# Query-key products by pairs of feature groups, one evacuation of the modulation rows, and a new issue order in a fused attention and token-MLP kernel

## The chip, the cores and the metric

The kernel runs on one core of one Trainium2 chip. The time is the device time of one execution in microseconds (us); lower is better. Five engines take part: TensorE (matrix products; its weight loads are listed apart as PEld), VectorE (DVE), ScalarE (ACT), GpSimd (POOL) and SyncE (SP), which issues most of the DMA transfers.

## The reference

A block of two halves over 2048 tokens of 512 features, in bf16. A vector `c` gives six rows of 512 by `silu(c) @ w_mod`: shift, scale and gate of each half.

```python
h = layernorm(x) * (1 + ca) + sa
x = x + ga * A(h, wqkv, wo)
h = layernorm(x) * (1 + cb) + sb
x = x + gb * B(h, w1, b1, w2, b2)
```

A is attention with 32 heads of 16 features in a dilated window: each token looks at itself and at the tokens 2, 4, ... 14 positions before it, eight in all; positions before the start are masked. B is an MLP over the tokens: for each feature, the 2048 tokens go through `w1` (2048 to 1792), a GELU, and `w2` back to 2048.

## The kernel before

**Tiles.** The tokens are cut into five chunks of 2, 4, 4, 4 and 2 tiles of 128 (`SIZES`), 256 or 512 tokens each. For a chunk, `build_chunk` (line 634) makes:

- the layernorm and its transpose (`ln1s`, `rstd1`, `n1`, then `tr` and `hT` on TensorE, or `xt` by DMA for chunks 2 to 4);
- the projections `qkv{chunk}_{0 q, 1 k, 2 v}{group}` and their evacuations `ev` from PSUM. The 16 features of a head are split into four groups of four; a partition holds one head and one feature of a group, and one group's q, k or v is a row of all the chunk's tokens;
- the query-key products `qk{chunk}_{group}` (line 767): VectorE multiplies q with eight shifted views of k, 8 x 512 = 4096 elements (2048 in the small chunks), into one of four `big` buffers. TensorE sums four features at a time with the matrix `group4` (`red`, line 775) into `psL`. `red` frees the `big` buffer;
- the softmax: `max` on VectorE, `sub` on TensorE, `exp` on ScalarE, `esum` on TensorE, `rcp` on ScalarE, `smB` on VectorE. Then four small DMAs (`a2`) bring the weights to the layout of the values, of which `vd` DMAs make shifted copies (`vD`);
- the value products `pv` on VectorE, also into `big` buffers, their sums `pvacc` on TensorE, the evacuation `oev`, the output projection `wo` and the residual `x1`;
- the second layernorm: `ln2q`, `rstd2`, `n2`, then `aff` (line 903): two VectorE instructions that multiply by the row 1 + cb and add the row sb; then a third normalisation, `ln3s`, `rstd3`, `h3`, which is B's own.

The MLP's first matrix is cut into sweeps (`mlp1_{part}_{column tile}_{first token tile}`) that start as soon as the first tiles of `h3` are there; partial sums are parked in SBUF (`park`, `padd`). `gelu`, then `mlp2_{token tile}`, `fin` and the stores follow.

**Modulation rows.** `build_mod_rows` (line 588) multiplies `silu(c)` with the columns of `w_mod`, a single row first (`modrow0`, the gate ga) and then three (`modrow1`: sb, cb, gb). The evacuation `mrows1` is two VectorE instructions: a copy of the three rows, and cb once more with 1 added (line 610). The rows go to DRAM (`st_row`) and come back spread over the partitions (`ld_row`).

**The order.** All operations are recorded first and then issued in the order of the list `ORDER` (line 192). Each engine runs its own operations in this order, and SyncE its DMAs. A token may name the engine (`:a` ScalarE, `:d` VectorE, `:p` GpSimd, `:s` SyncE). `:q` on a matrix product makes `mm` (line 541) issue it as four products of 32 output rows that run side by side in column tiles of the array, where it would else be one product over the whole array. `red`, `pvacc` and `modrow` are always in such tiles, `mlp2`, `qvb` and the transposes never. `fill:n` are n products without use. PSUM buffers (`ps`, six) and `big` buffers are given out in `schedule` (line 86): a buffer is held from the operation that allocates it to the last that frees it, and the one that has been free longest is taken.

All instructions are issued by a helper, so the profile gives line 143 for nearly all of them; they are told apart by the names of their tiles.

Of the kernel before, what the change touches and what calls it, by code (L numbers as in the profile page):

```python
# [42 lines left out]
class _Graph:  # L43
# [42 lines left out]
    def schedule(self):  # L86
# [4 lines left out]
        for pos, token in enumerate(ORDER.split()):  # L91
# [22 lines left out]
            if o.alloc is not None:  # L114
                p = o.alloc.pool
                o.alloc.i = min((freed[p][k], k) for k in range(self.pools[p]) if held[p][k] is None)[1]
                held[p][o.alloc.i] = o.alloc
# [54 lines left out]
def _t_tt2(n):  # L172
    return 0.154 + 0.00052 * n
# [25 lines left out]
ln1s12:a ev0_02:d ln1v13 qk0_2 qk0_0 qk0_1 qk0_3 ld_wqkv2 ld_wrow3 ld_x_4_14 qkv1_13:q qvb1 qkv0_20 ev1_10:a wsc2_2:a  # L199
ev1_00:a ln1s14 ev1_13:a qkv1_03:q red0_0 qkv0_22:q ln1v12 rstd1_3 ev1_03:a qvb_cp1:a qkv1_11:q red0_1 red0_2 red0_3  # L200
mask ld_wrow0 ld_wmod2 ld_wrow2 modrow0 qkv1_01:q ld_wrow1 ld_b1 qk1_0 max0 sub0:q qk1_3 ev0_20:a ev0_22:a ev1_11:a
ev1_01:a exp0 wsc1_3:a halo_v1:a qkv1_12:q biascols:q qkv1_02 ev1_02:a esum0:q rcp0 mrows0:a ev1_12:a qk1_1 wsc0_1:p
wsc1_1:p wsc0_2:p n1_7:p n1_9:p wsc1_2:p n1_6:p smB0 qk1_2 wsc2_3:a qkv1_22:q red1_0 qkv1_21:q modrow1 wsc2_0:a
a2_0_1:a ev1_22:a ev1_21:a ln1s15 nb1_3 red1_1 qkv1_23:q red1_2 red1_3 mrows1 max1 xt6 xt8 qkv1_20:q ev1_23:a wsc2_1:a
ev1_20:a qkv2_00:q qkv2_10:q vd0_2 vd0_3 vd0_1 ld_wo2 vd0_0 st_row0 a2_0_2:s a2_0_3:s a2_0_0:s ld_wo3 ld_row0 ld_wo0
n1_11:p n1_10:p pv0_1 pv0_2 pv0_3 pv0_0 sub1:q ev2_00:a biascols_cp:a exp1 ev2_10:a qkv2_03:q pvacc0_2 qkv2_11:q
fill:6:q qkv2_13:q esum1:q pvacc0_3 n1_12:a n1_13:a ev2_13:a ev2_03:a oev0_2:a pvacc0_0 pvacc0_1 rcp1 rstd1_4 oev0_0:a
qk2_0 woq_s smB1 qk2_3 qkv2_01:q qkv2_12:q qkv2_02:q ev2_11:a ev2_01:a a2_1_1:a ev2_12:a ev2_02:a qk2_1 qk2_2 wo1:q
x1_1:a wo0:q x1_0:a ln2q1 xt10 xt12 red2_0 qkv2_23:q qkv3_22:q qkv3_12:q vd1_0 st_row1 vd1_2 ev2_23:a ln2q0 rstd2_0
nb1_4 nb2_0 qkv2_21:q ev2_21:a red2_1 a2_1_2:s a2_1_0:s a2_1_3:s vd1_1 ld_row1 vd1_3 n1_14:p pv1_2 qkv3_13:q red2_2  # L210
red2_3 max2 qkv2_22:q n1_15:a ev3_13:a n2_1:a ev3_12:a ev2_22:a n2_0:a halo_v2:p qkv2_20:q sub2:q ev2_20:a exp2
pvacc1_2 qkv3_10:q halo_v3:a oev1_2:a ev3_10:a qkv3_02:q qkv3_20:q pv1_1 qkv3_01:q pvacc1_1 esum2:q ev3_02:a ev3_20:a
ev3_22:a aff0 pv1_0 qkv3_03:q qkv3_00:q pvacc1_0 pv1_3 oev1_1:a ev3_01:a rcp2 halo_k3:a smB2 ln3s0 qkv3_11:q oev1_0:a
pvacc1_3 ev3_11:a oev1_3:a qkv3_23:q fill:1:q wo5:q wo3:q qk3_2 qk3_1 ld_w1_0_0 ld_w1_0_512 vd2_3 xt14 vd2_2 vd2_1
a2_2_1:s a2_2_0:s a2_2_2:s vd2_0 a2_2_3:s wo4:q ln3s1 ev3_03:a ev3_00:a qk3_0 x1_3:a x1_4:a qk3_3 ln2q3 ln2q4 x1_5:a
ev3_23:a qkv4_22:q qkv3_21:q ev3_21:a wo2:q red3_0 x1_2:a qkv4_20:q fill:2:q red3_1 qkv4_00:q red3_2 ev4_22:a ln2q5
ln2q2 ev4_20:a rstd2_2 pv2_0 rstd2_4 red3_3 pvacc2_0 oev2_0:a pv2_3 qkv4_12:q ev4_12:a qkv4_02:q nb2_2 ev4_02:a n2_2:a
max3 sub3:q pvacc2_3 exp3 esum3:q oev2_3:a rstd3_0 pv2_2 nb2_4 pvacc2_2 qkv4_10:q rcp3 n2_5:a oev2_2:a n2_4:a pv2_1
pvacc2_1 fill:4:q oev2_1:a wo6:q wo7:q wo8:q wo9:q ev4_00:a smB3 n2_3:p vd3_3 ld_w1_0_896 vd3_1 vd3_0 a2_3_2:s a2_3_3:s
a2_3_0:s a2_3_1:s vd3_2 ld_w2_1 aff2 nb3_0 aff4 h3_1:p h3_0:p halo_v4:p ln3s3:a ln3s2:d ln3s4:d ln3v3 ln3v2 ln3v4  # L220
ln3s5:a ln3v5 pv3_1 x1_8:a x1_7:a x1_6:a rstd3_2 ev4_10:a h3_3 h3_2 mlp1_0_1_0 mlp1_0_2_0 mlp1_0_5_0:q mlp1_0_3_0:q
pvacc3_1 rstd3_4 nb3_4 x1_9:a pv3_2 pv3_3 pv3_0 h3_4:a h3_5:a oev3_1:a mlp1_0_2_2:q mlp1_0_1_2:q mlp1_0_0_0:q
mlp1_0_0_2:q mlp1_0_3_2:q mlp1_0_0_4:q mlp1_0_5_2:q mlp1_0_5_4:q mlp1_0_3_4:q mlp1_0_1_4:q pvacc3_2 mlp1_0_2_4:q ln2q9
ln2q6 park0_0:a park0_1:a ln2q7 park0_2:a oev3_2:a qk4_0 qk4_2 mlp1_0_4_0:q mlp1_0_4_2:q pvacc3_3 mlp1_0_6_0:q ln2q8
oev3_3:a mlp1_0_6_2:q pvacc3_0 mlp1_0_6_4:q mlp1_0_4_4:q oev3_0:a mlp1_0_7_0:q wo13:qn red4_0 rstd2_6 nb2_6 park0_3:a
qk4_1 x1_13:d n2_9:a n2_6:a park0_4:a wo12:q n2_8:p ld_w1_0_1152 ld_w1_0_1408 vd4_1 ld_w2_3 vd4_2 vd4_0 vd4_3 n2_7:d
qk4_3 wo11:q red4_1 red4_2 red4_3 ln2q13 x1_12:a ln2q12 park0_5:a x1_11:a rstd2_12 aff6 ln3s7:a mlp1_0_9_0 mlp1_0_9_2
mlp1_0_8_0 mlp1_0_9_4 wo10:n max4 nb2_12 sub4 exp4 park0_6:a ln3s9:d ln3s8:d ln3v8 ln3v9 esum4 ln3s6:d ln3v7 rcp4 ln3v6
smB4 rstd3_6 mlp1_0_7_2 mlp1_0_8_2 mlp1_0_10_0 mlp1_0_10_2 mlp1_0_12_0 mlp1_0_12_2 mlp1_0_8_4 mlp1_0_10_4 mlp1_0_7_4
mlp1_0_12_4 a2_4_1:s a2_4_2:s a2_4_3:s n2_13:p x1_10:d nb3_6 h3_8:d h3_6:d h3_7:d a2_4_0:a h3_9:a ln2q10 ln2q11  # L230
rstd2_10 n2_12:d aff12 mlp1_0_11_0 mlp1_0_11_2 mlp1_0_11_4 mlp1_0_8_6 mlp1_0_7_6 pv4_1 nb2_10 pv4_2 pv4_0 ln3s13
mlp1_0_9_6 mlp1_0_10_6 park0_7:a park0_8:a n2_10:a park0_9:a park0_10:a mlp1_0_12_6 mlp1_0_11_6 pvacc4_0 pvacc4_1
# [21 lines left out]
def kernel(  # L254
# [29 lines left out]
    INJ=(1,),  # L284
    CENT=((0, 14), (2, 0), (2, 12)),
# [44 lines left out]
    big_r = ring(NBIG, [P, NW * CM], BF, "big")  # L330
# [16 lines left out]
    epscol = T([P, 1], F32, "epscol")  # L347
    a1col = T([P, KT], F32, "a1col")
# [149 lines left out]
    def mk_consts():  # L498
        nc.gpsimd.memset(group4[:], 1.0)
# [88 lines left out]
    def build_mod_rows():  # L588
        for b_, (r0, nr) in enumerate(((0, 1), (1, 3))):
# [488 lines left out]
```

## Time and profile before

| | |
|---|---|
| Time, median of 3 runs | 199.04 us (198.99 to 199.58) |
| Profiled execution | 198.75 us |
| Its span, first to last instruction | 197.0 us |
| Mean granted TensorE clock | 0.997 |
| Matrix products / VectorE / ScalarE / GpSimd instructions | 2331 / 222 / 304 / 46 |
| Moved by DMA | 36.02 MB |

The span is what the profile shows; the time of the execution is 1.75 us longer. A busy TensorE isn't TensorE at its peak, since products are pipelined and their ends modelled. In a timeline row stand the start, the duration from the first start to the last end, the engine, the operation with its tiles and the count of instructions merged; in brackets is the idle time ahead of it and what ended it.

### The profile page before, as it was taken

Reading aid. Unit: us, or ns where it says so; the run is one execution under the profiler, and the core shown is the slowest. Engines: PE = TensorE matmul, PEld = TensorE weight load, DVE = VectorE, ACT = ScalarE, POOL = GpSimd, SP = SyncE. Lnnn points to the kernel's source line nnn. Section 1 sums busy time; section 2 is a strip of 40 time slices with the busy share of each in tenths; the row PEclk is TensorE's granted clock in tenths of the full one; section 3 lists DMA queues with packets and bytes.
Section 4 is the critical chain, followed back from the end, with each engine's and each line's share of the span. In section 5 each row is a group of like instructions: output and inputs, shape, how many; then the busy total and the mean of one; then the engine's idle time right before and its main releaser. Section 6 shows DMA issues by size and latency. Waiting matters only on the chain.

```text
span 197.0 us, 5568 instructions
## 1 busy us (share of the span) xinstructions
PE 185.8 (94%) x2331; PEld 99.5 (50%) x2343; DVE 157.3 (80%) x222; ACT 127.1 (64%) x304; POOL 22.8 (12%) x46
## 2 busy tenths in 40 slices
PE   3999999999999996899999999999999999999993
PEld 1476656565465674435554454444444444444462
DVE  2789999999999999999999999977550207864693
ACT  4799999898999999999997899735660000000000
POOL 4184003000500001130031000500000000000000
PEclk9999999999999999999999999999999999999998
DMA  5999695888997449180497494588999200144113
GB/s 156 357 355 341 226 259 137 101 201 253 302 303 268 149 144 322 34 218 14 136 245 208 91 255 97 157 273 177 290 348 339 61 0 15 38 130 99 53 53 107
DMA packets 53893, 36.02 MB, mean 183 GB/s; under 512 B 24428, under 2 KB 50668, under 8 KB 53868
## 3 DMA queue, kind: packets, MB, share of 16 engines
q1 hardware_dynamic: 52772, 35.27, 64.2%
q10 hardware_dynamic: 1096, 0.39, 0.8%
q8 instruction: 18, 0.29, 0.6%
q14 instruction: 7, 0.06, 0.1%
HBM read 22.55 MB, written 2.10 MB: 125 GB/s over the span
## 4 chain that ended last, share of the span: by engine, by line
PE 63%; DVE 21%; issue 5%; DMA 4%; SPq 3%; ACT 2%; DVEq 0%; ACTq 0%
PE psS L143 61%; DVE big L143 14%; DMA xx<-in_A_x_dram 4%; DVE h L143 4%; SPq L143 3%; PE psL L143 2%; DVE lsb L143 1%; DVE st L143 1%; ACT xx L143 1%; ACT junk L143 1%; DVE m L143 1%; DVE nb L143 0%; ACT k_f L143 0%; DVE woq L143 0%; ACT rs L143 0%
## 5 line engine op out<-in xcount | busy, mean ns | idle before, releaser
L143 PEld LDWEIGHTS <-wst 128*128 128x128 bf16 (+1 forms) x578 | 35.6, 101 | 32.7 <-issue 2.8
L143 PE MATMUL psS<-h,wst 128*32 128x512 bf16 (+1 forms) x350 | 50.1, 379 | 0.4 <-issue 0.2
L143 DVE TENSOR_TENSOR big<-a2sb,vD 128x4096 bf16<-128x4096 bf16 (+1 forms) x20 | 36.4, 1857 | 0.1
L143 DVE TENSOR_TENSOR big<-q_sb,k_f 128x4096 bf16<-128x4096 bf16 (+1 forms) x20 | 36.3, 1857 | 0.0
L143 PE MATMUL psS<-hT,w_qkv 128*32 128x512 bf16 (+1 forms) x576 | 29.0, 344 | 0.0
L143 DVE SCALAR_TENSOR_TENSOR h<-psS,bcol,rows_bc 128x512 f32<-128x512 f32 (+2 forms) x17 | 12.1, 709 | 21.2 <-PE psS L143 21.0
L143 PEld LDWEIGHTS <-w_qkv 128*32 128x32 bf16 (+1 forms) x618 | 21.2, 107 | 13.9
L143 PE MATMUL psS<-gT,big 128*128 128x512 bf16 x111 | 24.8, 379 | 0.1
L143 POOL TENSOR_SCALAR h<-xx,rs,nb 128x512 bf16<-128x512 bf16 x11 | 11.5, 1047 | 94.3 <-DVE nb L143 40.6
L143 PEld LDWEIGHTS <-big 128*128 128x128 bf16 x144 | 12.1, 98 | 13.8 <-DMA big<-in_w_mod_dram 0.5
L143 PE MATMUL psS<-woq,o_sb 128*32 128x512 bf16 (+1 forms) x220 | 16.7, 379 | 0.3 <-ACT o_sb L143 0.3
L143 ACT ACTIVATE gT<-psS,bcol 128x512 bf16<-128x512 f32 x14 | 8.9, 685 | 8.6 <-DVE psS L143 8.6
L143 DVE TENSOR_TENSOR psS<-psS,gT 128x512 f32<-128x512 f32 x14 | 9.4, 697 | 5.5 <-PE psS L143 5.5
L143 DVE TENSOR_TENSOR h<-h,xx 128x512 bf16<-128x512 f32 (+2 forms) x17 | 11.1, 652 | 2.6 <-DMA out_dram<-h 2.1
L143 PE MATMUL psS<-hT,wst 128*32 128x512 bf16 (+2 forms) x134 | 11.8, 355 | 0.2
L143 DVE TENSOR_TENSOR h<-h,rows_bc 128x1024 bf16<-128x1024 bf16 (+2 forms) x16 | 11.5, 718 | 0.5
L143 ACT ACTIVATE v_sb<-psS,qvb 128x512 bf16<-128x512 f32 (+1 forms) x20 | 11.1, 599 | 0.7 <-PE psS L143 0.7
L143 DVE BATCH_NORM_STATS2 st<-xx 128x6 f32<-128x512 bf16 x12 | 7.9, 681 | 4.5 <-DMA xx<-in_A_x_dram 4.5
L143 PEld LDWEIGHTS <-group 128*32 128x32 bf16 x288 | 7.7, 96 | 7.3 <-DVE big L143 1.7
L143 PE MATMUL psS<-big,group 128*32 128x512 bf16 (+1 forms) x160 | 9.9, 338 | 1.1 <-DVE big L143 0.8
L143 ACT ACTIVATE q_sb<-psS,qvb 128x512 bf16<-128x512 f32 (+1 forms) x18 | 10.6, 614 | 0.4 <-PE psS L143 0.3
L143 PEld LDWEIGHTS <-o_sb 128*32 128x32 bf16 (+1 forms) x220 | 7.0, 97 | 7.1 <-ACT o_sb L143 0.8
(106 smaller groups left out, 249.3 us busy)
## 6 DMA issues: line engine op xcount, KB each, us to landing
vD<-v_sb SPq DMA_DIRECT2D x12, 524.5 KB, 5.1
big<-in_B_w_dram SPq DMA_DIRECT2D x4, 896.0 KB, 8.3
vD<-v_sb SPq DMA_DIRECT2D x8, 268.5 KB, 2.5
wst<-in_B_w_dram SPq DMA_DIRECT2D x3, 640.0 KB, 4.4
out_dram<-h SPq DMA_DIRECT2D x15, 128.0 KB, 1.8
wst<-in_B_w_dram SPq DMA_DIRECT2D x2, 800.0 KB, 5.4
xx<-in_A_x_dram SPq DMA_DIRECT2D x6, 256.0 KB, 7.2
gT<-in_w_mod_dram SPq DMA_DIRECT2D x4, 384.0 KB, 7.6
```

The source lines that it names most:

```text
L143: r = fn(*a, **k)
```

## The change

- `qk` now takes two feature groups in one VectorE instruction (`QKP`, all chunks): 8192 elements in the chunks of 512 tokens, 4096 in the small ones. `big` becomes two double buffers, and a pair of the large chunks holds both halves of one until both its `red` are done. `schedule` gives out aligned pairs. The products are stored window by window with all tokens of the chunk in a row, so that `red` reads four runs of a window apart.
- `modrow1` gets four more products, ones times the identity, which add 1 to cb in PSUM; `mrows1` is one copy, and the order puts it on ScalarE.
- `aff` becomes two operations, `afm` (multiply) and `afs` (add), which the order can set apart.
- `ORDER` is new from chunk 0's query-key products on; the part before is unchanged. Tokens of ten `qk` instead of twenty stand in it. Among those that change engine: `mrows1` from VectorE to ScalarE; `ev0_20` and `wsc2_2` from ScalarE to VectorE; `n1_6`, `n1_7`, `n1_11`, `n1_14` from GpSimd to ScalarE; `n2_7` and `n2_9` to GpSimd. Other products have the `q` flag than before. The fillers behind the unchanged part are 26 units, before 13.

```diff
-                    held[o.frees.pool][o.frees.i] = None
-                    freed[o.frees.pool][o.frees.i] = pos
+                    z, k = o.frees.size, o.frees.i
+                    held[o.frees.pool][k:k + z] = [None] * z
+                    freed[o.frees.pool][k:k + z] = [pos] * z
...
+    QKP=(0, 1, 2, 3, 4, ),
+    PVP=(),
...
-    big_r = ring(NBIG, [P, NW * CM], BF, "big")
+    big_t = ring(NBIG // 2, [P, 2, NW * CM], BF, "big")
+    big_r = [big_t[i // 2][:, i % 2, :] for i in range(NBIG)]
...
+                    if (r0, r) == (1, 1):
+                        for dt_ in range(KT):
+                            nc.tensor.matmul(ps(s_)[32 * dt_:32 * dt_ + 32, r * P:(r + 1) * P],
+                                             lhsT=ones[:, 0:1].to_broadcast([P, 32]), rhs=ident[:], start=False, stop=True,
+                                             tile_position=(0, 32 * dt_))
...
-            if nr == 1:
-                copy2(rows, src_, P, False, [], [("mrows", b_)], f"mrows{b_}", frees=s_)
-            else:
-                def f_cp(rows=rows, src_=src_):
-                    nc.vector.tensor_copy(rows, src_())
-                    nc.vector.tensor_scalar_add(rows[:, 1, :], src_()[:, 1, :], 1.0)
-                add("dve", 0.8, f_cp, writes=[("mrows", b_)], frees=s_, name=f"mrows{b_}")
+            copy2(rows, src_, nr * P, False, [], [("mrows", b_)], f"mrows{b_}", frees=s_)
...
-        for dlo in range(4):
-            s_ = _Slot("big")
+        NQ = 2 if ch in QKP else 1
+        for d0 in range(0, 4, NQ):
+            s_ = _Slot("big", NQ * C // CM or 1)
...
+                return _ap(big_t[s_.i // 2][:, s_.i % 2, 0:1], [[NW * C, NQ], [C, NW], [1, C]])
+
+            def f(d0=d0, prod=prod):
+                qv = _ap(q_sb[:, d0, 0:1], [[C, NQ], [0, NW], [1, C]])
+                k0, k1 = k_c[:, 0, PAD:PAD + 1], k_c[:, 1, PAD:PAD + 1]
+                kv = _ap(k_c[:, d0, PAD:PAD + 1], [[k1.offset - k0.offset, NQ], [-DIL, NW], [1, C]])
+                nc.vector.tensor_tensor(prod(), qv, kv, op=ALU.mult)
...
+                            nc.tensor.matmul(psL[32 * jj:32 * jj + 32, hf, 0:WPM * SB], lhsT=group4[:],
+                                             rhs=pr[:, hf * WPM:(hf + 1) * WPM, jj * SB:(jj + 1) * SB], start=(dlo == 0),
+                                             stop=(dlo == 3), tile_position=(0, 32 * jj))
...
-                nc.vector.tensor_tensor(hv, hv, ab_bc[:].unsqueeze(1).to_broadcast([P, gn, D]), op=ALU.mult)
-                nc.vector.tensor_tensor(hv, hv, sb_bc[:].unsqueeze(1).to_broadcast([P, gn, D]), op=ALU.add)
+            for nm, row, rk, op_ in (("afm", ab_bc, "ab_bc", ALU.mult), ("afs", sb_bc, "sb_bc", ALU.add)):
```

The parts of the new order that the prediction speaks of, from the start of what changed, around the first MLP products, and around chunk 4's softmax:

```diff
+ln1s12:a ev0_02:d ln1v13 qk0_0 qk0_2 ld_wqkv2 ld_wrow3 ld_x_4_14 qkv1_01:q ev1_00:a n1_7:a qvb1 ev1_01:a qvb_cp1:a
+n1_6:a qkv0_20:q qkv0_22:q ev0_22:a qkv1_11:q red0_0 red0_1 red0_2 red0_3 mask ln1v12 rstd1_3 ev1_10:a ev1_11:a
+ev0_20:d wsc1_2:p n1_9:p wsc0_1:p wsc0_2:p wsc1_1:p wsc1_3:p nb1_3 wsc2_2:d max0 ld_wrow2 ld_wo0 ld_wrow0 ld_wmod2
+ld_wrow1 ln1s14 xt6 vd0_3 xt8 ld_wo2 ld_b1 vd0_0 vd0_1 qkv1_13:q sub0:q qkv1_02:q qkv1_03:q exp0 esum0:q modrow0
+qkv1_12:q ev1_02:a rcp0 ev1_13:a ev1_03:a mrows0:a st_row0 ev1_12:a qk1_0 smB0 qk1_2 qkv1_22:q n1_11:a qkv1_20:q
+qkv1_23:q a2_0_2:a ln1s15 red1_0 qkv2_11:q qkv1_21:q ev1_23:a ev2_11:a ev1_21:a n1_12:a ev1_22:a ev1_20:a red1_1
+qkv2_10:q red1_2 modrow1 red1_3 qkv2_00:q qkv2_01:q halo_v1:p n1_13:a wsc2_3:a ev2_10:a ev2_01:a n1_10:p a2_0_0:s
+a2_0_1:s a2_0_3:s vd0_2 ld_row0 ld_wo3 xt10 xt12 pv0_3 pv0_1 max1 sub1:q qkv2_13:q pv0_0 exp1 pvacc0_0 pvacc0_1 esum1:q
...
+vd3_3 ln3s3:a nb3_0 h3_1:p h3_0:p afs4 ln3s2:d ln3s4:d ln3v3 ln3v4 ln3v2 x1_7:a rstd3_2 x1_6:a ln3s5:a pv3_1 h3_3 h3_2
+ln3v5 mlp1_0_1_0 mlp1_0_2_0 mlp1_0_5_0 pvacc3_1 pv3_2 x1_9:a x1_8:a oev3_1:a rstd3_4 nb3_4 h3_5:d h3_4:a ln2q9 pv3_3
...
+nb2_6 n2_8:a n2_6:a park0_4:a park0_5:a mlp1_0_6_4:q mlp1_0_8_0:q red4_0 qk4_2 park0_6:a red4_1 wo13:qn mlp1_0_7_0:q
+mlp1_0_8_2:q red4_2 red4_3 x1_13:d wo12:q max4 sub4:q ln2q13 exp4 wo11:qn n2_7:p n2_9:p afm6 esum4 x1_12:a ln2q12 wo10
```

More of the change, by code (lines that the diff above doesn't have):

```diff
@@ L115, in schedule @@
                 p = o.alloc.pool
[L116 to L117 removed]
+                z = o.alloc.size
+                o.alloc.i = min((max(freed[p][k:k + z]), k) for k in range(0, self.pools[p] - z + 1, z)
+                                if held[p][k:k + z] == [None] * z)[1]
+                held[p][o.alloc.i:o.alloc.i + z] = [o.alloc] * z
             if o.frees is not None:
@@ L203 @@
[L203 to L207, printed above, removed]
@@ L218 @@
[L218 to L222, printed above, removed]
@@ L223 @@
[L223 to L232, printed above, removed]
```

111 lines of the change are left out of this document (59 added, 52 removed).

## The prediction

> **What bounds the kernel now.** I read the page first, for the engines' shares and the slices, then the chain of work that ended last in order of time, and then the busy times of each stretch that the chain separates.
>
> ```profile
> PE 185.8 (94%) x2331; PEld 99.5 (50%) x2343; DVE 157.3 (80%) x222; ACT 127.1 (64%) x304; POOL 22.8 (12%) x46
> ...
> DVE  2789999999999999999999999977550207864693
> ```
> ```profile
> 68.39 6.36 DVE big L143 x3
> ...
> 88.13 0.49 ACT k_f L143
> ...
> 88.67 10.66 PE psS L143 x192
> ```
> ```profile
> 16.50:39.90 23.40, 23.34 (x527) 14.06 (x531) 22.90 (x24) 22.18 (x51) 2.02 (x3) 1.00 0.78 207
> 39.90:62.00 22.10, 21.89 (x444) 12.44 (x440) 22.07 (x17) 21.02 (x49) 2.94 (x2) 1.00 1.00 266
> 62.00:88.67 26.67, 23.38 (x529) 14.02 (x522) 26.47 (x25) 25.83 (x70) 3.21 (x4) 1.00 0.60 182
> 88.67:117.00 28.33, 28.23 (x341) 14.30 (x346) 27.82 (x43) 25.84 (x65) 2.46 (x2) 1.00 0.61 148
> 150.00:190.50 40.50, 40.29 (x186) 18.41 (x189) 21.02 (x30) 0.00 (x0) 0.00 (x0) 1.00 0.26 77
> ```
>
> The columns of the stretches are the length, then busy time of PE, PEld, DVE, ACT and POOL, the granted clock and the DMA share. TensorE looks like the bound at 94%, but that is an average over two halves. From 16.5 to 88.67 us, the attention, VectorE is busy for 22.90 + 22.07 + 26.47 = 71.44 of 72.17 us, and the last stretch leaves TensorE 3.3 us of holes. From 88.67 us on, the token MLP, the chain stays on TensorE until 190.5 us. So the time is: the moment at which VectorE lets TensorE into the MLP, plus the TensorE work behind that moment, plus a tail that the change doesn't touch. ScalarE, at 25.83 of 26.67 us, has no room either. I take as the gate the first product of chunk 3's values (pv3_1) and the matmuls that sum it (pvacc3_1), since both orders have them there.
>
> **VectorE up to the gate.** The prices are start to start, because consecutive instructions overlap by some 0.07 us.
>
> ```profile
> 17.46 4.63 DVE L143 TENSOR_TENSOR big<-q_sb,k_f 128x2048 bf16<-128x2048 bf16 x4
> ...
> 32.10 0.55 DVE L143 CAST mrows<-psS 128x384 bf16<-128x384 f32 x1
> 32.69 0.29 DVE L143 TENSOR_SCALAR mrows<-psS 128x128 bf16<-128x128 f32 x1
> 33.26 1.22 DVE L143 TENSOR_REDUCE m<-psL 128x128 bf16<-128x1024 f32 x1 [0.28 <-PE psL L143]
> ...
> 61.65 8.89 DVE L143 TENSOR_TENSOR big<-q_sb,k_f 128x4096 bf16<-128x4096 bf16 x4
> ```
> ```profile
> L143 DVE TENSOR_TENSOR big<-q_sb,k_f 128x4096 bf16<-128x4096 bf16 x12 | 26.9, 2282 | 0.0
> ...
> L143 DVE TENSOR_SCALAR h<-xx,rs,nb 128x512 bf16<-128x512 bf16 x5 | 2.1, 411 | 0.1
> ...
> L143 DVE TENSOR_TENSOR q_sb<-psS,qvb 128x512 bf16<-128x512 f32 x1 | 0.7, 691 | 0.0
> ```
>
> Four products of 4096 elements take 8.89 us, so one starts (8.89 - 2.28) / 3 = 2.20 us after the last; of 2048, taking 1.22 us for the last one, (4.63 - 1.22) / 3 = 1.14. The 2048 more elements cost 1.06, so the fixed part is 1.14 - 1.06, about 0.07 us. That is all that a pair saves: elements are not fewer, and a pair of 4096 should take 4.34 us against 4.41. No row shows 8192 elements; the bounds are 0 and 0.15 us per pair (0.15 by whole durations: 2 x 1.22 - 2.28, rounded down), and I take 0.07, the row of back-to-back instructions. Eight pairs stand before the gate: **-0.56**. The second evacuation (mrows1) leaves VectorE, from 32.10 to 32.69 + 0.29 = 32.98: **-0.85** with its gaps. In return the order gives VectorE ev0_20, by the evacuation of the same form 0.69 - 0.07 = **+0.62**, and wsc2_2, a 512-element scaling at 0.41 - 0.07 = **+0.34**. One small aggregate (ln3v5) goes behind the gate, some **-0.1**. The split of aff into afm and afs has the same two instructions. Sum: **-0.55 us**. The 0.28 us that the maximum of chunk 1 waits should go too, since two value products of chunk 0 now lie before it.
>
> mrows1 lands on ScalarE at about the 0.55 of its cast, and four normalisations move there from GpSimd, while ev0_20, two weight scalings, one normalisation and a halo copy leave. Summed by durations less overlap, the queue is within 1 us of its old length at each softmax, so I put it at nothing; without VectorE's cover it would cost up to that 1 us. The added identity products are four, of 128 columns, side by side: under 0.1 us.
>
> **What waits instead.** Two places of the new order look late.
>
> ```profile
> 22.61 1.03 PE L143 MATMUL psS<-hT,wst 128*32 128x512 bf16 x16
> 23.47 0.82 PE L143 MATMUL psL<-big,group 128*32 128x512 bf16 x12
> 24.22 0.23 PE L143 MATMUL psL<-mask,ident 32*32 32x128 bf16 x1
> ```
> ```profile
> 24.48 0.69 DVE L143 TENSOR_REDUCE m<-psL 128x64 bf16<-128x512 f32 x1
> ...
> 29.49 0.42 DVE L143 TENSOR_TENSOR lsb<-lsb,rb 128x512 bf16<-128x512 bf16 x1
> ...
> 34.55 4.63 DVE L143 TENSOR_TENSOR big<-a2sb,vD 128x2048 bf16<-128x2048 bf16 x4
> ```
> ```profile
> 29.25 0.56 SPq L143 DMA_DIRECT2D scratch<-mrows  x1
> 29.94 2.01 SPq L143 DMA_DIRECT2D a2sb<-lsb  x3
> ```
> ```profile
> a2sb<-lsb SPq DMA_DIRECT2D x6, 32.0 KB, 3.6
> ```
>
> First, max0 needs TensorE's mask product. TensorE has one projection group less ahead of it (23.47 - 22.61 = 0.86 us), so max0 can start at 24.48 - 0.86 = 23.6. VectorE, which used to put a product of chunk 1 in between, now arrives at 17.46 + 2 x 2.20 + 0.14 + 0.62 + 0.08 + 0.34 = 23.0. Wait: 0 to 0.6, I take **+0.5**. The whole of chunk 1's first pair is behind it. Second, pv0 needs the softmax of chunk 0 through a DMA. smB0 ends at 23.6 + 0.61 + 4.34 + 0.42 = 29.0. SyncE first issues st_row0 (0.56) and then three of the four pieces at 0.67 each, so the third issue starts at 30.9 at the latest, or at 30.3 if st_row0 is out before. Landing takes 3.6 us by the median, but before it took at most 34.55 - 31.28 = 3.3 us, as pv0 did not wait there: 33.6 to 34.2. VectorE is there after one pair, at 33.3, where the old order still had three more instructions. Wait: 0 to 1.0, I take **+0.4**; behind it wait max1 and everything of chunk 1. So up to the gate -0.55 - 0.28 + 0.5 + 0.4 = **+0.07**.
>
> **TensorE behind the gate.**
>
> ```profile
> 88.67 0.61 PE L143 MATMUL psS<-big,group 128*32 128x512 bf16 x8 [0.29 <-ACT k_f L143]
> 89.21 4.50 PE L143 MATMUL psS<-h,wst 128*32 128x512 bf16 x80
> 93.52 0.62 PE L143 MATMUL psS<-big,group 128*32 128x512 bf16 x8
> ...
> 101.51 0.83 PE L143 MATMUL psL<-big,group 128*32 128x512 bf16 x12
> 102.28 1.90 PE L143 MATMUL psS<-h,wst 128*128 128x512 bf16 x7
> ```
>
> A step of 512 columns in four column tiles takes (93.52 - 89.21) / 20 = 0.215 us. Before, four first MLP products stood ahead of pvacc3_1; now three do, and mlp1_0_3_0, two steps, goes behind: **+0.43**. The order also changes which products run in column tiles (the q flags). Three groups from 101.51 would end at 101.51 + 0.645 = 102.16, and the next, full-array product starts at 102.28: a change of form costs 0.12. Counted in the two orders, there are 3 changes behind the gate before and 7 after; one of these falls into the wait at the gate, so 3 x 0.12 = **+0.36** (0 to 0.5). The ten further changes ahead of the gate, 1.2 us, and 13 more filler units go into TensorE's 3.3 us of holes; without these they'd be paid.
>
> The Trainium skill, TensorEngine Tiling (Array Packing), section Key Properties, says that a change of tiling mode drains TensorE. By that rule the last product's whole 0.38 us would have to pass, 0.165 more than a step, an estimate of 0.5 in place of 0.36; the row shows the smaller price.
>
> ```profile
> wst<-in_B_w_dram SPq DMA_DIRECT2D x2, 800.0 KB, 5.4
> ```
>
> The tightest load of the MLP, ld_w1_2_0 of this size, has 5.4 us to landing; its buffer comes free with mlp1_1_5_10, and 29 steps of 0.215, 6.2 us, lie between that and its first use. It costs nothing, with 0.8 us of cover. The tail keeps its last two output tiles in the same order: nothing. Sum: +0.07 + 0.43 + 0.36 = **+0.86**. The profiled execution took 198.75 us (span 197.0 and 1.75 around it) and would come to 199.6; against the median of the runs, 199.04, I predict **199.9 us**.
>
> **The rivals.**
>
> ```profile
> 76.20 0.62 PE L143 MATMUL psL<-m,nident 128*32 128x512 bf16 x8 [1.04 <-DVE m L143]
> ...
> 78.05 0.63 PE L143 MATMUL psS<-lsb,ident 128*32 128x128 bf16 x32 [0.80 <-ACT lsb L143]
> ...
> 80.68 0.61 PE L143 MATMUL psS<-big,group 128*32 128x512 bf16 x8 [0.69 <-DVE big L143]
> ```
> ```profile
> 49.79 2.28 DVE L143 TENSOR_TENSOR big<-a2sb,vD 128x4096 bf16<-128x4096 bf16 x1
> ```
> ```profile
> 49.96 2.76 POOL L143 TENSOR_SCALAR h<-xx,rs,nb 128x512 bf16<-128x512 bf16 x1 [16.09 <-ACT v_sb L143]
> ...
> 104.87 0.77 POOL L143 TENSOR_SCALAR h<-xx,rs,nb 128x512 bf16<-128x512 bf16 x1 [4.66 <-DVE nb L143]
> ```
> ```profile
> L143 ACT ACTIVATE junk<-xx,sums 128x512 bf16<-128x512 bf16 x14 | 10.1, 723 | 0.2
> ```
>
> *Faster: the lead reaches the gate.* The two waits don't come, which is so if the softmax pieces land within a pair, 4.3 us, of smB0. Then VectorE gains 0.55 + 0.28 = 0.83, and TensorE, let in that much earlier, has done the moved steps and the changes in its holes of 1.04, 0.80 and 0.69 us: 199.04 - 0.83 = 198.2. If half of the two longest holes closes as well, 0.9 less, 197.3. For it speaks that these holes are there; against it that VectorE, not the order of TensorE, makes them.
>
> *No change.* The waits come, and TensorE's 0.79 us disappears in holes, or the other way about: 199.1 or 199.0. That the pairs don't do what they say belongs here too: at no saving per pair the forecast would move by 0.56, to 200.5. That they'd lose the fast rate I leave out: their innermost step stays one element of bf16, as in the products with vD, which cost the same 2.28.
>
> *Slower still: GpSimd behind a pair.* GpSimd's normalisation at 49.96 took 2.76 us while VectorE's product of 2.28 ran, against 0.77 at 104.87. In the new order n2_7 and n2_9 of chunk 2 both go to GpSimd just as VectorE starts the second pair of chunk 4 (2.20 us), and afm6 needs both: 2.20 + 2 x 0.77 = 3.7 us after the start, where VectorE arrives after 2.20 + 0.61 + 0.61 = 3.4. That 0.3, and the 0.72 us of a ScalarE square (ln2q11) that now stands ahead of h3_8, hit h3_6 to h3_9, which TensorE takes as soon as they are made: +1.0, so 200.9. It decides from the point where h3_8 comes later than mlp1_0_7_6 reaches it. The Trainium skill, SBUF — State Buffer, section SBUF: two separate sides, has the rule for this: the port pair that VectorE and GpSimd share is an exclusive lock for a whole instruction. The two rows above agree with it.
>
> **How the numbers follow.** Forecast 199.9: 0.34. Faster, 198.2: 0.33. No change, 199.1: 0.17. Slower still, 200.9: 0.16. The lower end takes in the faster case with most of the closed holes, 197.4; the upper end the slower case with half a microsecond more for the softmax pieces (1.0 in place of 0.4, rounded down), 201.4. Within 0.3% (0.6 us) is what a measurement of this kernel can't tell from no change; 0.05 of the forecast's chance falls in there. So faster 0.33, same 0.17 + 0.05 = 0.22, slower 0.29 + 0.16 = 0.45.
>
> **What would show it.** Each step has its place in the new profile: pairs at 4.34 us start to start; VectorE idle before the first maximum and before the first product with vD, by TensorE and by a DMA; the gate near 88.7 us; TensorE's work behind the gate longer by 0.8 us. I'm wrong if the gate opens before 88 us, or if TensorE's stretch behind it is as long as before; GpSimd's case shows as TensorE idle between 105 and 115 us.

## The result, and the profile after

The changed kernel takes **201.54 us** (median of 4 runs, 201.14 to 202.04) against 199.01 for the kernel before (198.44 to 199.58): ratio 1.0128, 95% interval 1.0091 to 1.0165. A second set of six runs gave 201.56 us and 1.0114 (1.0094 to 1.0134). Three executions of all that follow, at a lower granted clock, took over 1.5% longer than the fastest of the same kernel, and times and ratios leave them out. The forecast, 199.9, had the direction; the loss is three times as large, and 201.54 lies outside the range. The profiled execution of after took 201.54 us, 2.79 more than that of before.

The page of after, shares of the engines (VectorE has 11 instructions fewer, TensorE 35 more):

```profile
PE 188.0 (94%) x2366; PEld 97.4 (49%) x2366; DVE 156.4 (78%) x211; ACT 125.6 (63%) x298; POOL 24.7 (12%) x49
```

Busy times of after in the first stretch, columns as in the prediction:

```profile
16.50:39.90 23.40, 21.64 (x497) 13.37 (x499) 21.20 (x20) 20.41 (x46) 3.14 (x6) 1.00 0.91 203
```

In before VectorE was busy for 22.90 of these 23.40 us; now it has 2.2 us of holes. VectorE's own rows (start, duration, idle ahead of it) show the largest of these and the largest of a later stretch:

```profile
18.02 4.47 DVE L146 TENSOR_TENSOR big<-q_sb,k_f 128x4096 bf16<-128x4096 bf16 x2
...
23.93 0.69 DVE L146 TENSOR_REDUCE m<-psL 128x64 bf16<-128x512 f32 x1
24.53 4.42 DVE L146 TENSOR_TENSOR big<-q_sb,k_f 128x8192 bf16<-128x8192 bf16 x1
28.86 0.42 DVE L146 TENSOR_TENSOR lsb<-lsb,rb 128x512 bf16<-128x512 bf16 x1
...
35.69 2.40 DVE L146 TENSOR_TENSOR big<-a2sb,vD 128x2048 bf16<-128x2048 bf16 x2 [1.86 <-DMA a2sb<-lsb]
...
42.55 0.68 DVE L146 TENSOR_TENSOR lsb<-lsb,rb 128x1024 bf16<-128x1024 bf16 x1
...
63.71 8.75 DVE L146 TENSOR_TENSOR big<-q_sb,k_f 128x8192 bf16<-128x8192 bf16 x2
...
83.44 0.69 DVE L146 TENSOR_TENSOR lsb<-lsb,rb 128x1024 bf16<-128x1024 bf16 x1 [0.79 <-ACT rb L146]
```

The pairs do what was said: 8.75 - 4.42 = 4.33 us start to start. The first value product (pv0_3) waits 1.86 us for the softmax pieces, and smB3 0.79 us for ScalarE. SyncE's queue says why the pieces are late:

```profile
22.10 2.20 SPq L146 DMA_TRANSPOSE hT<-h  x1
24.49 0.63 SPq L146 DMA_DIRECT2D vD<-v_sb  x1
25.22 1.32 SPq L146 DMA_TRANSPOSE hT<-h  x1
26.59 0.69 SPq L146 DMA_DIRECT2D woq<-in_A_wo_dram  x1
27.33 0.56 SPq L146 DMA_DIRECT2D b_t<-in_B_b_dram  x1
27.94 2.10 SPq L146 DMA_DIRECT2D vD<-v_sb  x2
30.14 0.56 SPq L146 DMA_DIRECT2D scratch<-mrows  x1
30.81 2.86 SPq L146 DMA_DIRECT2D a2sb<-lsb  x3
```
```profile
L146 SPq DMA_DIRECT2D a2sb<-lsb x3: 617/685/1448, 30.8 to 32.2; - x3
```

From 22.10 us on it has no gap: seven entries, 7.50 us in all, ahead of the row's store. The pieces' values were ready at 28.86 + 0.42 = 29.28 us, but their issues start at 30.81 and the last one at 32.2. In before, the entries in the same place were seven too, but of 5.98 us, and done when the values came at 29.49 + 0.42 = 29.91 us:

```profile
22.96 2.96 SPq L143 DMA_TRANSPOSE hT<-h  x2
26.03 1.89 SPq L143 DMA_DIRECT2D vD<-v_sb  x3
27.96 0.60 SPq L143 DMA_DIRECT2D woq<-in_A_wo_dram  x1
28.61 0.53 SPq L143 DMA_DIRECT2D vD<-v_sb  x1
```

So the queue is late by how long its entries hold it, not by their number. A second profile of the same kernel, further down (`after_again`), shows another cause for the same late issue.

The chain of after, in order of time, runs over ScalarE from 64.72 us to smB3, where that of before had VectorE's products; behind it TensorE has it:

```profile
64.72 0.45 ACT o_sb L146
...
83.10 0.32 ACT rb L146
...
84.92 12.57 PE psS L146 x127
```

For a balance, the same points in before, VectorE's smB1 and smB3 and TensorE's last group of mlp2_13, and TensorE in after:

```profile
42.44 0.68 DVE L143 TENSOR_TENSOR lsb<-lsb,rb 128x1024 bf16<-128x1024 bf16 x1
...
80.54 0.68 DVE L143 TENSOR_TENSOR lsb<-lsb,rb 128x1024 bf16<-128x1024 bf16 x1
```
```profile
187.34 5.50 PE L143 MATMUL psS<-gT,wst 128*128 128x512 bf16 x42
```
```profile
90.53 0.61 PE L146 MATMUL psS<-big,group 128*32 128x512 bf16 x8
91.04 6.45 PE L146 MATMUL psS<-h,wst 128*32 128x512 bf16 x82
97.52 1.10 PE L146 MATMUL psS<-big,group 128*32 128x512 bf16 x16
...
190.41 5.49 PE L146 MATMUL psS<-gT,wst 128*128 128x512 bf16 x42
```

| stretch | before | after | difference |
|---|---|---|---|
| up to smB1; by then after has done one product of chunk 2 (2.20) less | 42.44 | 42.55 + 2.20 | +2.31 |
| smB1 to smB3, without that product | 38.10 + 2.20 | 40.89 | +0.59 |
| smB3 to the sum of pv3_1 (the gate) | 8.13 | 7.09 | -1.04 |
| gate to the last group of mlp2_13 | 98.67 | 99.88 | +1.21 |
| from there to the end of the execution | 11.41 | 11.13 | -0.28 |

The sum is +2.79. From smB3 on the two kernels take the same time within 0.2 us: what is won up to the gate is lost again behind it. All of the loss is there at smB3.

### The profile page after: what moved, and what is told of

It reads as the page before. It is cut to its first block, busy times and chain, and to the rows that moved or that the text cites. A ratio compares the mean times of both kernels' runs of the same rounds, so it can differ in the third digit from the quotient of the medians.

```text
span 199.8 us, 5621 instructions
## 1 busy us (share of the span) xinstructions
PE 188.0 (94%) x2366; PEld 97.4 (49%) x2366; DVE 156.4 (78%) x211; ACT 125.6 (63%) x298; POOL 24.7 (12%) x49
## 4 chain that ended last, share of the span: by engine, by line
PE 72%; ACT 11%; SPq 5%; DMA 4%; DVE 4%; issue 2%; POOL 0%; ACTq 0%; DVEq 0%
PE psS L146 70%; SPq L146 5%; ACT junk L146 3%; DMA xx<-in_A_x_dram 2%; DVE h L146 2%; PE psL L146 2%; ACT v_sb L146 2%; DMA woq<-in_A_wo_dram 2%; ACT h L146 1%; ACT xx L146 1%; ACT q_sb L146 1%; ACT o_sb L146 1%; ACT lv L146 1%; DVE m L146 1%; ACT hT L146 1%
## 5 line engine op out<-in xcount | busy, mean ns | idle before, releaser
L146 PEld LDWEIGHTS <-wst 128*32 128x32 bf16 (+1 forms) x746 | 35.8, 100 | 32.4 <-issue 2.9
L146 PE MATMUL psS<-h,wst 128*32 128x512 bf16 (+1 forms) x512 | 50.8, 379 | 0.0
L146 DVE TENSOR_TENSOR big<-q_sb,k_f 128x8192 bf16<-128x8192 bf16 (+1 forms) x10 | 35.5, 3562 | 0.1
L146 PE MATMUL psS<-hT,w_qkv 128*32 128x512 bf16 (+3 forms) x504 | 29.8, 344 | 0.0
L146 PEld LDWEIGHTS <-w_qkv 128*32 128x32 bf16 (+1 forms) x546 | 20.4, 107 | 15.3 <-issue 1.7
L146 DVE SCALAR_TENSOR_TENSOR h<-psS,bcol,rows_bc 128x512 f32<-128x512 f32 (+2 forms) x17 | 12.1, 710 | 18.7 <-PE psS L146 18.2
L146 POOL TENSOR_SCALAR h<-xx,rs,nb 128x512 bf16<-128x512 bf16 x11 | 12.5, 1138 | 52.6 <-DVE nb L146 52.4
L146 ACT ACTIVATE h<-xx,nb,rs 128x512 bf16<-128x512 bf16 x15 | 11.8, 812 | 0.0
L146 PEld LDWEIGHTS <-o_sb 128*32 128x32 bf16 (+1 forms) x136 | 5.7, 96 | 10.7 <-ACT o_sb L146 3.4
L146 DVE TENSOR_TENSOR h<-h,rows_bc 128x1024 bf16<-128x1024 bf16 (+2 forms) x16 | 10.8, 684 | 0.2
L146 ACT ACTIVATE v_sb<-psS,qvb 128x512 bf16<-128x512 f32 (+1 forms) x18 | 10.4, 612 | 0.4 <-ACT h L146 0.3
```

The lines of the kernel that those rows point to most:

```text
L146: r = fn(*a, **k)
```

## The experiments

Each was timed beside runs of the kernel before on the same chip; ratios are to that kernel, with 95% intervals. Theory: the new order's queues on SyncE and ScalarE cost the time, and the changes of form on TensorE. First rival: the coarser pairs do.

**Pairs taken apart, new order kept** (`e1_unpaired`)

```diff
-    QKP=(0, 1, 2, 3, 4, ),
+    QKP=(),
...
-... qk0_0 qk0_2 ...
+... qk0_0 qk0_1 qk0_2 qk0_3 ...
```

> The changed kernel with every pair of query-key products taken apart again into two instructions, in the same new order. Theory (the loss comes from the new order's queues, on SyncE and ScalarE, and from changes of tile form on TensorE; a pair saves its 0.07 us): nothing won by it, 201.5 to 202.1 us beside the 201.5 of the changed kernel, and the same 1.9 us wait of the first product with vD. Rival one (the pairs are the loss: the coarser product keeps TensorE's sums and the buffers waiting): at least 1 us faster than the changed kernel, 200.5 us or less.

201.62 us, 1.0132 (1.0106 to 1.0159): the same as with pairs. The rival falls. In its VectorE rows the wait for the pieces is shorter by 0.54 us. Four of the eight pairs stand ahead of it, so 0.28 us of that can be their saving; the other four stand ahead of smB3, whose wait for ScalarE is 0.63 us here in place of 0.79:

```profile
34.97 2.40 DVE L146 TENSOR_TENSOR big<-a2sb,vD 128x2048 bf16<-128x2048 bf16 x2 [1.32 <-DMA a2sb<-lsb]
```

**Pairs alone, old order** (`e2_pairs_in_old_order`)

```diff
-... qk2_0 woq_s smB1 qk2_3 qkv2_01:q ... qk2_1 qk2_2 ...
+... qk2_0 woq_s smB1 qkv2_03:q ... qk2_2 ...
...
-... qk3_2 qk3_1 ... qk3_0 ... qk3_3 ...
+... qk3_2 ... qk3_0 ...
```

> The kernel before, its order kept as far as it goes, with pairs in chunks 0, 2, 3 and 4 (chunk 1 stays in single products; groups 1 and 3 of chunk 2 trade places so that a pair is ready early). Theory: 6 pairs of 8 before the gate save 0.07 us each, 0.4 us, less what the later start of the first sum costs: 198.4 to 199.3 us. Rival one: 200.0 us or more, with TensorE waiting for VectorE's products in each chunk.

205.93 us, 1.0343 (1.0311 to 1.0376), 204.42 in the profiled execution: the theory fails, and the time is on the rival's side, far above its 200.0. The rival's reason, TensorE waiting for VectorE, isn't the first one. In the VectorE rows it is VectorE that waits:

```profile
40.93 4.42 DVE L146 TENSOR_TENSOR big<-q_sb,k_f 128x8192 bf16<-128x8192 bf16 x1 [1.60 <-ACT q_sb L146]
...
46.41 0.68 DVE L146 TENSOR_TENSOR lsb<-lsb,rb 128x1024 bf16<-128x1024 bf16 x1
49.00 4.43 DVE L146 TENSOR_TENSOR big<-q_sb,k_f 128x8192 bf16<-128x8192 bf16 x1 [1.91 <-ACT q_sb L146]
```

A pair needs two groups evacuated before it starts, and smB1, behind it in VectorE's queue, comes 3.97 us later than before. Of these about 2.1 us are the second group's product, which now stands ahead of smB1, and 1.60 are the wait; the next pair waits another 1.91. So pairs have a price, and a new order must be there to pay it; in the new order these waits are gone.

**The modulation rows alone, old order** (`e3_rows_in_old_order`): the four identity products and the single copy, on ScalarE.

> The kernel before with only the second part of the change: cb's 1 added by TensorE, and one evacuation of the three rows, left on ScalarE or VectorE as the old order's token has it free, where VectorE's 0.85 us goes. Theory (VectorE leads up to the gate): 0.3 to 0.8 us faster than before, 198.2 to 198.7 us. Rival: ScalarE, which takes the evacuation, leads by as much, and the time stays within 0.3 us of 199.0.

198.85 us, 0.9993 (0.998 to 1.0007): the rival. The maximum of chunk 1 starts at 33.26 as before, and what was 0.28 us of waiting is now 1.12:

```profile
33.26 1.22 DVE L143 TENSOR_REDUCE m<-psL 128x128 bf16<-128x1024 f32 x1 [1.12 <-PE psL L143]
```

The taker is TensorE rather than ScalarE, and it takes the whole 0.84 us.

**Softmax pieces first in SyncE's queue** (`e4_softmax_dma_first`)

```diff
-... xt8 ld_wo2 ld_b1 vd0_0 vd0_1 ... mrows0:a st_row0 ... qk1_2 qkv1_22:q ... a2_0_0:s a2_0_1:s a2_0_3:s vd0_2 ld_row0 ld_wo3 xt10 ...
+... xt8 vd0_0 vd0_1 ... mrows0:a ... qk1_2 a2_0_0:s a2_0_1:s a2_0_3:s st_row0 qkv1_22:q ... vd0_2 ld_row0 ld_wo2 ld_wo3 ld_b1 xt10 ...
```

> The changed kernel with the last three pieces of chunk 0's softmax weights moved in SyncE's queue ahead of the store of the gate row, the load of wo's last part and that of b1. Theory: the wait of VectorE's first product with vD (1.86 us) shrinks by a third to all of it, and as VectorE leads from there to softmax 3, 0.5 to 1.5 us of it reach the end: 200.0 to 201.0 us. Rival two (ScalarE's queue at softmax 3 is the bound and takes back what VectorE wins before it): the wait shrinks, the end stays at 201.2 to 201.6 us.

199.78 us, 1.0033 (1.002 to 1.0046): **1.8 of the 2.5 us come back**, from the order of a few DMAs alone. Its VectorE rows:

```profile
34.10 2.35 DVE L146 TENSOR_TENSOR big<-a2sb,vD 128x2048 bf16<-128x2048 bf16 x2
...
40.38 1.23 DVE L146 TENSOR_TENSOR woq<-woq,rows_bc 128x2048 bf16<-128x2048 bf16 x1 [0.52 <-DMA woq<-in_A_wo_dram]
```

The wait of 1.86 us is gone; a new one stands at the product on woq, whose load went back in the same queue. The edit takes two things away at once, time that the store and the loads hold the queue and the load of wo ahead of the pieces, so by itself it doesn't tell which of them made the pieces late.

**One form of product** (`e5_one_form`): `:q` on everything from qkv1_01 to mlp1_0_13_0, off behind it.

> The changed kernel with one form of product as far as the order lets it: from the second projection of chunk 1 on, all projections and MLP products run in column tiles until mlp1_0_13_2, then over the whole array, so that one change of form is left behind the gate instead of seven, and fewer ahead of it. Theory (a change costs TensorE 0.12 us): 0.7 us faster than the changed kernel, 200.5 to 201.0 us. Rival: changes of form are hidden or the four small products cost what the changes save: 201.3 us or more.

200.81 us, 1.009 (1.0069 to 1.0111), in the expected range. But the profile doesn't bear out the reason: from the gate (90.11) to the last group of mlp2_13 (189.82) it takes 99.71 us, 0.17 less than after. The changes around mlp1_0_0_2 went, and pvacc3_3 waits for a PSUM buffer instead, which a park frees:

```profile
97.23 1.10 PE L146 MATMUL psS<-big,group 128*32 128x512 bf16 x16 [0.25 <-ACT gT L146]
```

**ScalarE relieved** (`e6_scalar_relief`): `n2_4:a` becomes `n2_4:d`, `n2_5:a` goes behind rcp3.

> The changed kernel with ScalarE's queue ahead of softmax 3 relieved: n2_4 on VectorE, and n2_5 behind rcp3. Theory (ScalarE leads there, by the 0.79 us that the multiplication smB3 waits for rb): that wait goes, less 0.35 for n2_4 on VectorE, and 0.3 to 0.8 us reach the end: 200.7 to 201.3 us. Rival (SyncE's queue around 30 us is the whole of the loss ahead of the gate, and the wait at smB3 only passes it on): 201.4 to 201.8 us.

200.88 us, 1.0088 (1.0062 to 1.0113). smB3 waits no longer, and starts 0.27 us sooner, at 83.17; but in this profile the first value product already started 0.36 us sooner, at 35.33, so the stretch between them isn't shorter. The intervals of `e5_one_form` and `e6_scalar_relief` overlap that of the changed kernel, so a gain of half a microsecond isn't settled.

**All three** (`e7_all_three`)

> The changed kernel with the three edits together: softmax pieces first in SyncE's queue, one form of product, and ScalarE relieved ahead of softmax 3. If the three add up (1.8 us measured for the first, 0.7 and 0.5 expected of the others): 198.4 to 199.0 us, level with or ahead of the kernel before. If only the first counts: 199.6 to 200.0 us.

199.53 us, 1.0031 (1.0014 to 1.0047): only the first counts.

**The price of a change of form** (`e8_many_forms`): in the kernel before, `:q` on every second mlp1_1 and mlp1_2.

> The kernel before with every second product of the MLP's later sweeps (mlp1_1 and mlp1_2, 34 operations, where TensorE never waits) in column tiles: 32 changes of form more, nothing else. At 0.12 us a change: +3.8 us, 202.5 to 203.2 us. At the price of a drained product, 0.165 us: +5.3 us, 204.3 us. If changes cost nothing: 199.0 us.

202.46 us, 1.0175 (1.0152 to 1.0199). TensorE's rows of it, gate and last group:

```profile
88.28 0.62 PE L143 MATMUL psS<-big,group 128*32 128x512 bf16 x8
...
190.69 5.50 PE L143 MATMUL psS<-gT,wst 128*128 128x512 bf16 x42
```

102.41 us against 98.67, and 37 changes behind the gate against 3: the 17 products make 34 more, not 32. So 3.74 / 34 = **0.110 us a change**, where TensorE has no hole. By the rule of the Trainium skill (TensorEngine Tiling (Array Packing), section Key Properties), a change drains the array; the runs agree that it costs, at less than a whole product's passing, which would be 0.165 us beyond a step (0.38 - 0.215).

**The changed kernel again** (`after_again`)

> The changed kernel once more, unedited, as the yardstick for the others. The profiles show that one form of product and ScalarE's relief change the stretch from the first query-key product to the end by less than 0.3 us, while their medians lie 0.7 us below that of the changed kernel. If that 0.7 us is the spread between sets of runs (the first product starts at 17.2 to 18.2 us in runs of one and the same order): 200.8 to 201.2 us here. If it is a gain of the two edits: 201.4 to 201.7 us again.

201.56 us. Its first query-key product starts at 17.38, 0.64 us sooner than in the first profile, and yet:

```profile
35.71 2.40 DVE L146 TENSOR_TENSOR big<-a2sb,vD 128x2048 bf16<-128x2048 bf16 x2 [1.87 <-DMA a2sb<-lsb]
```

The first value product starts 0.02 us apart in the two: VectorE's lead went into a wait for k_f (0.69 us, ahead of the pair before it) and for the pieces. SyncE sets this start, and the first product's 0.56 us against before is no part of the loss. But here the queue wasn't late. Its rows, its wait between 29 and 33 us, and the chain:

```profile
29.10 0.56 SPq L146 DMA_DIRECT2D scratch<-mrows  x1
29.78 3.01 SPq L146 DMA_DIRECT2D a2sb<-lsb  x3
```
```profile
SPq L146 <- DMA woq<-in_A_wo_dram: 1.0, 1, 1.0
```
```profile
26.61 5.55 DMA woq<-in_A_wo_dram
...
32.18 0.61 SPq L146
```

The row's store goes out at 29.10 us, a microsecond sooner than in the first profile, and the first piece at 29.78. The third is issued at 32.18 all the same: SyncE stands for 1.0 us until the load of wo (ld_wo2), issued at 26.61, has landed, though the piece reads nothing of wo. Six profiles have the pieces and the loads in this order on SyncE (`after`, `after_again`, `e1_unpaired`, `e5_one_form`, `e6_scalar_relief`, `e11_own_piece_first`). Three show this wait, of 0.9 to 1.0 us; in the other three wo has landed and the queue itself is late. The third issue comes between 31.6 and 32.2 us in all six. Why a piece waits for that load isn't shown.

**Another order of the three pieces** (`e11_own_piece_first`): `a2_0_3:s` ahead of `a2_0_0:s`.

> The changed kernel with nothing but the order of three DMAs on SyncE's queue changed: of the softmax pieces of chunk 0, the one that the first product with vD reads (a2_0_3) is issued first instead of last; the queue ahead of them stays as full. Theory (the product waits for its own piece, issued last of a late queue, at 32.2 us): it is issued 1.4 us earlier, the wait of 1.86 us falls to 0.2 to 0.6 us, and about 1.2 us reach the end: 199.9 to 200.6 us. Rival (all pieces land late because the transfers ahead of them are still under way): the wait stays over 1.3 us, the time within 0.4 us of the changed kernel.

201.11 us, 1.0109 (1.0085 to 1.0133), the wait 1.94 us. The expectation had the kernel wrong: each value product reads all four pieces, so the last one counts, whichever it is, and it was issued at 31.8, behind the same wait for wo:

```profile
L146 SPq DMA_DIRECT2D a2sb<-lsb x3: 610/617/685, 29.4 to 31.8; - x3
```

**TensorE's work put back** (`e10_mended`): pieces first; mlp1_0_3_0 and x1_8 ahead of pvacc3_1; `:q` on five products around mlp1_0_0_2, off in the later sweeps.

> The changed kernel with the softmax pieces ahead of the loads, and TensorE's work behind the gate put back: mlp1_0_3_0 ahead of pvacc3_1 (x1_8 earlier on ScalarE for it), the five MLP products around mlp1_0_0_2 in column tiles, the later sweeps over the whole array. Theory: the gate stays 0.5 us ahead of that of the kernel before, counted from the first query-key product, and the 1.2 us behind the gate fall to 0.2 to 0.5 us: 198.6 to 199.1 us. Rival (what is taken from TensorE there turns into waits for PSUM buffers): 199.5 us or more.

200.25 us, 1.0075 (1.0046 to 1.0103): nothing over the pieces alone. Behind the gate TensorE takes 99.07 us in place of 100.06, but the gate is as much later, 89.93 in place of 88.97: the work only changed sides. The product on woq starts where it did with the pieces alone (40.38), though VectorE came to it 0.9 us sooner, about as much as this profile's first product started sooner (17.36 in place of 18.23):

```profile
40.47 1.23 DVE L146 TENSOR_TENSOR woq<-woq,rows_bc 128x2048 bf16<-128x2048 bf16 x1 [1.55 <-DMA woq<-in_A_wo_dram]
```

**The kernel before with rows and fewer changes** (`e13_before_mended`): `:q` from mlp1_0_9_0 to mlp1_0_11_6.

> The kernel before with the second part of the change (one evacuation of the three rows) and two changes of form fewer behind the gate: everything from mlp1_0_9_0 to mlp1_0_11_6 in column tiles. Theory: two changes at 0.11 us, 0.2 us, and the 0.15 us that the rows brought by the profile: 198.5 to 198.8 us. Rival: products in column tiles cost what the changes save: 198.8 to 199.2 us.

200.76 us, 1.0077 (1.006 to 1.0093): slower by far more than the rival had. A new wait in TensorE's rows:

```profile
116.51 0.62 PE L143 MATMUL psS<-big,group 128*32 128x256 bf16 x16 [0.50 <-DVE big L143]
```

The pieces of chunk 4's softmax were issued at 108.4 us, as with the rows alone (108.5), but the first value product behind them started at 112.89 us, having waited 0.90 for them, in place of 112.00. Why, and why the stretch behind the last group of mlp2_13 is 0.9 us longer as well, stays open.

**Loads in SyncE's idle time** (`e14_loads_in_gap`; `e15_gap_and_pieces_first` has the pieces ahead of st_row0 as well)

```diff
-... ld_wrow1 ln1s14 xt6 vd0_3 xt8 ld_wo2 ld_b1 ... ld_row0 ld_wo3 xt10 ...
+... ld_wrow1 ln1s14 ld_wo2 ld_b1 ld_wo3 xt6 vd0_3 xt8 ... ld_row0 xt10 ...
```

> The changed kernel with three loads (two pieces of wo, and b1) moved in SyncE's queue ahead of its first transpose (xt6), where it stands idle from 17.8 to 22.1 us; the softmax pieces stay behind the gate row's store. Theory (SyncE's queue is the loss ahead of the gate): the queue ahead of the pieces is 1.2 us shorter, the wait of the first product with vD falls from 1.86 to 0.4 to 0.9 us, the product on woq doesn't wait: 200.0 to 200.6 us. Rival: 201.2 us or more.

> The same, and the pieces of chunk 0's softmax ahead of the gate row's store. Theory: neither the first product with vD nor the product on woq waits for a DMA; the 0.5 us and more that remained of the woq wait go too: 198.8 to 199.4 us. Rival (ScalarE's queue at softmax 3, or TensorE's longer work behind the gate, keeps it): 199.6 to 200.0 us, as with the pieces first alone.

201.57 us, 1.0144 (1.012 to 1.0167), and 201.97 us, 1.0181 (1.0139 to 1.0224): neither brings what was expected. The first isn't told apart from the changed kernel; the second loses all that the pieces first had brought. SyncE was idle from 17.8 to 22.1 us in after, but the DMA engines (last but one column) were full:

```profile
17.00:20.00 3.00, 3.00 (x52) 1.54 (x49) 3.00 (x6) 2.97 (x8) 1.07 (x2) 1.00 1.05 379
```

In `e14_loads_in_gap` the transpose behind the loads held SyncE for 4.09 us. That isn't what VectorE then waits for, since chunk 1's keys don't come through this transpose. The value products find their pieces landed; the wait has moved ahead of them, to chunk 1's second pair, and behind it stand ScalarE and TensorE, which stops for 1.77 us between the 29th and the 30th of the 32 products of chunk 0's esum:

```profile
22.07 4.09 SPq L146 DMA_TRANSPOSE hT<-h  x1
```
```profile
26.61 0.40 PE L146 MATMUL psS<-lsb,ident 128*32 128x64 bf16 x29
28.78 0.21 PE L146 MATMUL psS<-lsb,ident 128*32 128x64 bf16 x3 [1.77 <-issue]
```
```profile
29.03 0.22 ACT L146 ACTIVATE ls<-psS 128x64 f32<-128x64 f32 x1 [2.21 <-PE psS L146]
```
```profile
31.29 4.42 DVE L146 TENSOR_TENSOR big<-q_sb,k_f 128x8192 bf16<-128x8192 bf16 x1 [1.29 <-ACT k_f L146]
```

"issue" means that the profile shows nothing that TensorE waited for. With the loads in the gap this stop is there in all four profiles (1.77, 3.28, 2.33 and 2.13 us), always at this product; in `after` it is absent and in `after_again` 0.42 us. So the loads bring it; how isn't shown. On top of e15, relieving ScalarE (`e16_gap_and_relief`) gave 201.64 us, 1.0152 (1.0121 to 1.0183), and taking the pairs apart (`e17_gap_unpaired`) 202.38, 1.0177 (1.0157 to 1.0198); with such a stop ahead neither tells anything.

**Pieces, then wo, then the row** (`e18_pieces_then_wo`): as with the pieces first, with ld_wo2 and ld_wo3 ahead of st_row0.

> The changed kernel with the softmax pieces of chunk 0 first in SyncE's queue, then the last two pieces of wo, and only then the gate row's store; b1 stays behind. Theory (the product on woq waits for wo's load, issued at 34.6 us when the store and its way back go first): wo is issued at 31.7 us, the wait of 0.5 to 1.6 us goes, 0.4 to 1.0 us better than with the pieces first alone: 198.8 to 199.4 us. Rival (something else holds the stretch from softmax 3 on): 199.6 us or more.

200.54 us, 1.0088 (1.0067 to 1.011); with ScalarE relieved (`e19_pieces_wo_relief`) 201.02, 1.011 (1.0086 to 1.0135). The theory fails: wo is there, and the product on woq waits for its other operand, the gate row, and starts at the same time:

```profile
40.41 1.23 DVE L146 TENSOR_TENSOR woq<-woq,rows_bc 128x2048 bf16<-128x2048 bf16 x1 [1.12 <-DMA rows_bc<-scratch]
```

In its profile smB3 (81.89) and the last group of mlp2_13 (189.06) are where the pieces alone have them (81.88 and 189.03); why its median is 0.8 us higher is open. No version beat the kernel before by more than can be measured.

## Why the prediction went wrong

- **Pairs, 4.34 us each:** measured 4.33. The 0.56 us that eight of them save ahead of the gate don't arrive: the kernel takes as long without pairs, and its waits for the pieces and at smB3 are shorter (1.32 in place of 1.86 us, 0.63 in place of 0.79).
- **The rows, -0.85:** wrong as a gain of the path. In the old order TensorE had the next wait, 0.28 us, in view in the quoted row, and took the rest.
- **The first maximum, +0.5:** didn't come. It started at 23.93, 5.91 us behind the first product, where 6.14 was forecast, without a wait for TensorE.
- **The softmax pieces, +0.4 (0 to 1.0): the step that failed.** The prediction let the third issue start "at 30.9 at the latest": it began with st_row0 as soon as the values were ready, at 29.0, took the queue to be free then, and let nothing come between the pieces. The values came at 29.28, the third issue at 32.2, and the wait was 1.86. In the profile of after, seven earlier entries kept SyncE until 30.04 us and the third piece followed; in that of after_again the queue was free in time, and the third piece waited 1.0 us for ld_wo2 to land. Adding the entries up with their durations in before would not have been enough: 2.96 for the transposes, 1.89 for three vD, 0.60 for wo and some 0.6 for b1 are 6.05 us, which from 22.10 end near 28.5 with the short gaps, still ahead of the values. In after the seven held the queue for 7.94 us with their gaps. The range of 0 to 1.0 had no room for such a spread, nor for a wait behind an earlier load. Moving wo, b1 and the row's store behind the pieces gave back 1.8 us: that these entries are the cause is shown, and the two ways in which they act are read from the profiles. Much of what remains seems to hang on this queue as well: the product on woq starts between 40.0 and 40.5 us in all five versions that reorder it behind early pieces, whether its last operand is wo or the gate row. In the mended version VectorE would be 0.2 us ahead of before at smB1 without the 1.55 us there (41.61 + 2.20 - 42.44 - 1.55); no run removes that wait, so this part is argued.
- **The gate, "near 88.7 us":** it opened at 90.53. The faster rival needed the pieces to land within a pair, 4.3 us, of smB0; they took 35.69 - 29.28 = 6.4.
- **ScalarE's queue, nothing, up to 1 us without cover:** within the bound. smB1 to smB3 costs 0.59 us more, with smB3 waiting 0.79 for ScalarE. That relieving ScalarE brings it back isn't shown.
- **TensorE behind the gate, +0.79:** measured +1.21. The price of a change (0.12, measured 0.110) was about right, and mlp1_0_3_0 stands behind the gate as counted; but the two changes around mlp1_0_0_2 cost 0.46 together (91.04 to 97.52 for 28 steps of 0.215), twice that price, and two in the later sweeps come to 0.2 by it. Yet this is no loss of its own: the gate came 1.04 us sooner behind smB3, and taking work from behind it moved the gate. The balance should have been cut at smB3.
- **The tail, nothing:** -0.28.
- **GpSimd behind a pair** did slow down, to 3.43 us for two normalisations in place of 2 x 0.77, but TensorE had other work: it was busy for all of 105 to 115 us. The row of after:

```profile
100.90 3.43 POOL L146 TENSOR_SCALAR h<-xx,rs,nb 128x512 bf16<-128x512 bf16 x2 [12.90 <-DVE nb L146]
```

## What to carry to other kernels

Before you cost a moved DMA, write down the queue that it stands in from its last idle moment, entry by entry, with the longest holds that the trace shows beside the usual ones; a transfer is issued when the queue reaches it, not when its data are ready. Then ask the trace what each entry waits for: here it was an earlier load in the same queue that had nothing to do with it. A saving on the leading engine counts only up to the next wait that the profile already shows, and an edit that moves work across a chosen point shows as a gain on one side and a loss on the other: cut the balance where the two orders have done the same work.

## What the hardware showed

An idle issue queue isn't an idle DMA system: three loads put into 4 us of SyncE's idle time, at a DMA share of 1.05, brought nothing where 1 us was expected back. In the four profiles with them the first transpose behind them held SyncE for 4.09 to 4.78 us (1.34 to 2.20 in eleven other profiles of the new order), and TensorE stopped in one place for 1.77 to 3.28 us. On SyncE a plain DMA mostly held the queue for 0.5 to 0.7 us, but single ones for 1.25 and 1.45, and a DMA could stand for 1.0 us until another one, seven entries earlier, had landed. A change of form costs TensorE 0.110 us, mean of 34 in a stretch without holes. The first query-key product starts between 17.3 and 18.2 us in profiles that share the order up to it, so a single profile's start is no term of a sum.
